# TensorE's eight passes over K and V written as one loop in the program, with V at one place and K turned into two fixed buffers

## The chip, the core and the metric

The kernel runs on one core of a Trainium2 chip. The metric is the device time of one execution in microseconds (us). Before the change it is 400.53 us (median of 3 runs, 400.43 to 400.56). All inputs lie in HBM and are read once; the result is one row of 1024 numbers.

## The reference, cut to what matters

A single token `x` (1 x 1024) goes through a layernorm, and the normed row `xn` then through two blocks whose results are added to `x`. Block A is attention of 32 query heads over a cache of 65536 keys in 4 groups (8 heads share a group's K and V); block B is a small MLP.

```python
q = (xn @ wq).reshape(B, Sq, Hq, Dh).transpose(0, 2, 1, 3)          # 32 heads of 128
scores = jnp.einsum("bhqd,bhkd->bhqk", q, k) * (Dh ** -0.5)         # k, v: 4 groups x 65536 x 128
o = jnp.einsum("bhqk,bhkd->bhqd", softmax(scores), v)
A = o.transpose(0, 2, 1, 3).reshape(B, Sq, Hq * Dh) @ wo
h = gelu(layernorm(xn) @ w1); x1 = xn + shifted(h) @ w2             # one token: every shift brings in zeros
B = x1 + gelu(layernorm(x1) @ w3) @ w4
return x + A + B
```

All arrays are bf16. K and V are 67.1 MB each, the weights together some 36 MB; the profile counts 169.87 MB read from HBM.

## The kernel before, in words

The kernel writes its program through a recorder (`Program`). Each call like `dve.transpose(...)` or `prog.load(...)` adds one `Op` to a list, with the regions that it reads and writes. `plan` then finds for each op which earlier ops it must wait for, and `emit` writes the instructions for every engine in that order: each engine executes its own ops in the order of the list, and waits on semaphores. A wait is attached to the instruction itself (the last of several; the others become separate wait instructions ahead of it, as do all waits of an instruction that accumulates). Because all goes through the recorder, VectorE's and ScalarE's instructions stand under one line in the profile (L82), loads from HBM under L89, weight loads of TensorE under L102, bf16 matmuls under L106 and f32 matmuls under L116 and L122.

The work is eight **turns** (u = 0 to 7), two for each of the four groups (g = u // 2, b = u % 2). A turn takes half a group's cache: 32768 keys, an 8.39 MB tile of K and as large a tile of V, each laid out as 128 partitions by 32768 bf16. A turn consists of:

- `scores(u)`: for each of four quarters of the K tile, VectorE transposes the quarter in 32 x 32 blocks, in place (128 x 4096 words), and TensorE runs 16 matmuls of it against `qdiag`, which holds the group's queries on its diagonal blocks, into `sc` (128 x 2048 f32 in PSUM). All 64 matmuls accumulate into the same four banks.
- `maxima(u)`: VectorE takes the maximum of each row of `sc`; TensorE turns the column of maxima into a row (`turn32`), VectorE reduces over the rows of one head, TensorE turns the result back, VectorE copies it to `nball`.
- `weights(u)`: ScalarE computes the exponential of `sc` into `p_sb` with the sums in `lall`, and VectorE transposes `p_sb`.
- `values(u)`: TensorE runs 64 matmuls of `p_sb` against the V tile into `oacc`.
- After the first turn of a group ScalarE copies `oacc` to `og` (`first_rows`). In the second turn VectorE weighs the two halves (`group_weights`, `group_rows`), a pair of f32 matmuls of `ol` against `selx` gathers the heads, and four small VectorE steps put the group's result into `oT`. These last steps stand on VectorE ahead of the next turn's first transpose.

Ahead of the turns stand the layernorms and the products with `wq`, `w3`, `w1` and `w2`; behind them the product with `wo` (64 matmuls from `oT`) and the one with `w4`, whose tile comes in five pieces, and the output.

All large loads are issued by SP in one queue, in the order wq, w3, w1, w2, K0, V0, K1, V1, ... K7, V7, wo, w4. SBUF holds three **slots** of 128 x 32768 bf16; the n-th tile of that stream has slot n % 3, and a load is recorded where the tile three places ahead in the stream has had its last use (`freed`):

```python
stream = ["wq", "w3", "w12"] + [(kind, u) for u in range(NU) for kind in "KV"] + ["wo", "w4"]
tiles = {it: slots[i % 3] for i, it in enumerate(stream)}
...
n = stream.index(it) + 3
if n < len(stream):
    load(stream[n])
```

So V of turn u+1 is issued when the scores of turn u are done, and K of turn u+2 when the values of turn u are done. The functions that the change touches are `Op`, `Program`, `load`, `scores`, `maxima`, `weights`, `values`, `first_rows`, `group_rows` and the loop over the turns at the end.

Of the kernel before, what the change touches and what calls it, by code (L numbers as in the profile page):

```python
# [14 lines left out]
P = 128  # L15
# [24 lines left out]
class Op:  # L40
    def __init__(self, engine, emit, reads, writes, alone=False, transfer=False):
        self.engine, self.emit, self.alone, self.transfer = engine, emit, alone, transfer
        self.reads = [region(a) for a in reads]
        self.writes = [region(a) for a in writes]
        self.waits = []
        self.awaited = False


class Program:

# [3 lines left out]
    def __init__(self, nc):  # L54
        self.nc = nc
        self.engines = {"pe": nc.tensor, "dve": nc.vector, "act": nc.scalar, "pool": nc.gpsimd, "sp": nc.sync}
        self.ops = []
        self.held = {}
        self.sems = []

    def add(self, op):
        for key in [k for k, (_, r) in self.held.items() if any(meet(r, w) for w in op.writes)]:
            del self.held[key]
        self.ops.append(op)
        return op

# [57 lines left out]
    def plan(self):  # L124
# [4 lines left out]
        for n, op in enumerate(self.ops):  # L129
# [21 lines left out]
            if e == "pool" and last_pool is not None:  # L151
                needs(last_pool, True)
            picked = sorted(need.values(), key=lambda o: o.n)
# [22 lines left out]
            for r in op.reads:  # L176
                readers.setdefault(r[0], []).append((r, op))

# [4 lines left out]
    def emit(self, first, last):  # L183

        if not hasattr(self, "queue_sems"):
            self.queue_sems = {e: self.sem(f"done_{e}") for e in ("pe", "dve", "act", "pool")}
            self.values = {e: 0 for e in self.engines}
        for n, op in list(enumerate(self.ops))[first:last]:
            e = self.engines[op.engine]
            waits = [(o.sem, o.value) for o in op.waits]  # L190
            ahead = waits if op.alone else waits[:-1]
            for s, v in ahead:
                e.wait_ge(s, v)
            ins = op.emit()
            if waits and not op.alone:
                ins.wait_op(waits[-1][0], waits[-1][1], "sem-ge")
            if op.transfer:
                op.sem, op.value = self.sem(f"landed_{n}"), 16
                ins.then_inc(op.sem, 16)
            elif op.awaited:  # L200
                self.values[op.engine] += 1
                op.sem, op.value = self.queue_sems[op.engine], self.values[op.engine]
                ins.then_inc(op.sem, 1)
# [3 lines left out]
def kernel(  # L207
# [42 lines left out]
    slots = [sb(f"slot{i}", [P, ROW], BF16) for i in range(3)]  # L250
# [34 lines left out]
    stream = ["wq", "w3", "w12"] + [(kind, u) for u in range(NU) for kind in "KV"] + ["wo", "w4"]  # L285
    tiles = {it: slots[i % 3] for i, it in enumerate(stream)}

    def load(it):
        t = tiles[it]
        if it == "wq":  # L290
            prog.load("sp", t[:], A_wq.rearrange("(p c) n -> p (c n)", c=DC))
# [5 lines left out]
        elif it == "wo":  # L297
            prog.load("sp", t[:], A_wo.rearrange("(p j) n -> p (j n)", p=P))
        elif it == "w4":
            w4_v = B_w4.rearrange("(m c) n -> m c n", c=FC)  # L300
            c0 = 0
            for n in W4_PIECES:
                prog.load("sp", t[:, c0 * D:(c0 + n) * D], w4_v[:, c0:c0 + n, :].rearrange("p c n -> p (c n)"))
                c0 += n
        else:
# [3 lines left out]
            prog.load("sp", t[:], cache[0, g, b * UKEYS:(b + 1) * UKEYS, :].rearrange("(p ct) d -> p (ct d)", p=P))  # L309

    def freed(it):

        n = stream.index(it) + 3
        if n < len(stream):
            load(stream[n])
# [24 lines left out]
    pool.memset(g_col[:], 0.0)  # L340

# [55 lines left out]

    def compute_wq():
        wt = tiles["wq"][:].rearrange("p (c h a i) -> p c h a i", c=DC, a=4, i=32)
        row_matmul(xn_rep, lambda c, i, a: wt[:, c, 16 * i:16 * (i + 1), a, :], (512, 512))  # L400
        freed("wq")
# [10 lines left out]
    def place_queries(g):  # L412
        for a in range(4):
            at = slice(32 * a, 32 * a + 32)
            pool.tensor_copy(
                out=qdiag[at, LEAD:].rearrange("p (x c) -> p x c", x=4)[:, :, 32 * a:32 * a + 8],
                in_=qx[at, :, 8 * g:8 * g + 8])

    def compute_w3():
# [3 lines left out]
        freed("w3")  # L423
# [6 lines left out]
    def compute_w12():  # L430
# [10 lines left out]
        freed("w12")  # L441

    W = ROW // SETS
# [12 lines left out]
    def scores(u):  # L456
        g, b = divmod(u, NB)
        if b == 0:
            place_queries(g)
        t = tiles["K", u]  # L460
        cols = t[:].rearrange("p (s u k b x r) -> p s u k b x r", u=SUBS, s=SETS, k=16, b=2, r=2)
        for s in range(SETS):
            words = t[:, W * s:W * (s + 1)].bitcast(F32)
            dve.transpose(out=words, in_=words)
            for b2 in range(2):
                for r in range(2):
                    c0 = LEAD + P * (2 * b2 + r) - 8 * s
                    for e in range(SUBS):
                        pe.mm(sc[:, e, :], qdiag[:, c0:c0 + P], cols[:, s, e, :, b2, :, r],
                              s == 0 and b2 == 0 and r == 0, s == SETS - 1 and b2 == 1 and r == 1)  # L470
        freed(("K", u))

    def maxima(u):
        g, b = divmod(u, NB)
        dve.reduce_max(out=mx[:], in_=sc[:].rearrange("p e n -> p (e n)"), axis=AX.X)
        at = next_pm()
        pe.turn32(at[0:1, 0:P], mx[:, 0:1], ident_f[:])
        dve.tensor_reduce(out=m8[:], in_=at[0:1, 0:P].rearrange("o (j h) -> o h j", h=8), axis=AX.X, op=ALU.max)
        dve.tensor_scalar(out=rep[:].rearrange("o (j h) -> o j h", h=8),
                          in0=m8[:].unsqueeze(1).to_broadcast([1, P // 8, 8]), scalar1=-SCALE, scalar2=None, op0=ALU.mult)  # L480
# [3 lines left out]
    def weights(u):  # L484
# [3 lines left out]
        dve.transpose(out=p_sb[:], in_=p_sb[:])  # L488

    def values(u):  # L490
        vt = tiles["V", u][:].rearrange("p (s u t d) -> p s u t d", u=SUBS, s=SETS, t=16)
# [5 lines left out]
        freed(("V", u))  # L497

    def first_rows():
        act.copy(out=og[:], in_=oacc[:])  # L500
# [8 lines left out]
    def group_rows(g):  # L509
        at = next_pm()  # L510
# [4 lines left out]
        pe.mm32(at[:, 0:DH + 1], selx[:], ol[:], True, True)  # L515
# [11 lines left out]
    for u in range(NU):  # L527
        g, b = divmod(u, NB)
        scores(u)
# [7 lines left out]
        else:  # L537
            group_rows(g)

# [77 lines left out]
```

## Time and profile before

| what | value |
|---|---|
| median of 3 runs | 400.53 us |
| the profiled execution, its own time | 400.43 us |
| its span, first to last instruction | 399.1 us |
| mean granted TensorE clock | 0.798 |
| TensorE busy (matmul) | 221.0 us, 55% |
| VectorE busy | 210.2 us, 53% |
| ScalarE busy | 27.6 us, 7% |
| HBM read | 169.87 MB, 426 GB/s over the span |
| one 128 x 4096 transpose of K | 4411 ns, 32 of them |
| one matmul of `scores` | 512 of them, 128.4 us busy in all |

The page names engines PE (TensorE matmul), PEld (TensorE weight load), DVE (VectorE), ACT (ScalarE), POOL (GpSimd) and SP. A timeline line gives the start within the span, the length, the engine, the line of the kernel, the operation, and in brackets how long the engine had been idle before and what released it. The lines of the queue that loads (SPq) give the time of the issue, not of the landing. The chain of waits goes from the last instruction back to what released it, and shows each piece with its start and its length; a DMA piece runs from the issue to the landing, so it includes the time that the transfer stands in the queue behind others.

### The profile page before, as it was taken

To read this page: it belongs to the slowest core of one execution; us is meant where nothing else is said; L and a number is where in the kernel's file an instruction comes from. 1 tells how busy PE (TensorE), PEld (TensorE's weight loads), DVE (VectorE), ACT (ScalarE), POOL (GpSimd) and SP (SyncE) were. 2 spreads that over 40 slices of the span, in tenths; PEclk is the share of its full clock that TensorE was granted. 3 is DMA by queue.
4 is the path that set the end of the run, shared out by engine and by line. 5 is a ranking of instruction groups with operands and counts; after the bars stand their busy time and mean duration, and the time that the engine had idled before them with its cause. 6 is when DMAs were issued, how large, how long until landed. Compare 5 with 4: busy or idle time off the path is not lost.

```text
span 399.1 us, 2559 instructions
## 1 busy us (share of the span) xinstructions
PE 221.0 (55%) x1360; PEld 45.5 (11%) x890; DVE 210.2 (53%) x156; ACT 27.6 (7%) x35; POOL 6.2 (2%) x29
## 2 busy tenths in 40 slices
PE   0250970592669246822874387429552946393586
PEld 0210010000201010011001100101010102010233
DVE  0520010975096549643963696359439932793411
ACT  1010030002000200020002000200010010002000
POOL 2000000000000000000000000000000000000000
PEclk9996895697659686968795679678966986597789
DMA  8989999999999999999999999999999999999996
GB/s 342 479 388 417 471 420 427 421 460 466 422 420 427 420 429 427 460 453 427 415 427 420 434 440 447 448 427 420 427 429 434 440 447 435 427 420 427 402 442 256
DMA packets 3760, 170.03 MB, mean 426 GB/s; under 512 B 419, under 2 KB 421, under 8 KB 678
## 3 DMA queue, kind: packets, MB, share of 16 engines
q1 hardware_dynamic: 3744, 169.87, 98.7%
q8 instruction: 9, 0.15, 0.1%
q14 instruction: 1, 0.01, 0.0%
q10 hardware_dynamic: 6, 0.00, 0.0%
HBM read 169.87 MB, written 0.00 MB: 426 GB/s over the span
## 4 chain that ended last, share of the span: by engine, by line
DMA 56%; DVE 21%; PE 17%; another core or an unknown queue 2%; ACT 2%; issue 0%; SPq 0%; POOLq 0%
DMA slot<-in_A_k_cache_dram 42%; DVE slot L82 15%; PE sc L106 12%; DMA slot<-in_B_w_dram 9%; DMA slot<-in_A_wq_dram 5%; PE oacc L106 4%; DVE p_sb L82 2%; DVE mx L82 2%; ACT p_sb L82 2%; PE pm L122 1%; DVE m L82 0%; DVE rep L82 0%; DVE nball L82 0%; DVE x_halves L82 0%
## 5 line engine op out<-in xcount | busy, mean ns | idle before, releaser
L82 DVE STREAM_TRANSPOSE slot<-slot 128x4096 f32<-128x4096 f32 x32 | 139.4, 4411 | 52.4 <-DMA slot<-in_A_k_cache_dram 52.3
L106 PE MATMUL sc<-slot,qdiag 128*128 128x512 bf16 x512 | 128.4, 410 | 69.7 <-DVE slot L82 69.6
L106 PE MATMUL oacc<-slot,p_sb 128*32 128x512 bf16 x512 | 44.9, 528 | 37.5 <-DVE negmg L82 18.8
L82 DVE STREAM_TRANSPOSE p_sb<-p_sb 128x2048 bf16<-128x2048 bf16 (+2 forms) x10 | 20.8, 2085 | 38.9 <-ACT p_sb L82 38.8
L82 DVE TENSOR_REDUCE mx<-sc 128x1 f32<-128x2048 f32 x8 | 18.3, 2292 | 29.7 <-PE sc L106 29.7
L102 PEld LDWEIGHTS <-qdiag 128*128 128x128 bf16 x128 | 13.0, 102 | 180.8 <-issue 180.8
L82 ACT ACTIVATE p_sb<-sc,nball 128x2048 bf16<-128x2048 f32 x8 | 15.7, 1967 | 250.7 <-DVE nball L82 250.7
L102 PEld LDWEIGHTS <-p_sb 128*32 128x32 bf16 x512 | 17.0, 128 | 62.1 <-issue 19.7
L106 PE MATMUL sc<-slot,ln_rep_b 128*32 128x512 bf16 (+1 forms) x80 | 16.2, 827 | 9.4 <-DMA slot<-in_B_w_dram 9.1
L82 DVE SCALAR_TENSOR_TENSOR og<-oacc,wb,og 128x512 f32<-128x512 f32 x4 | 3.0, 750 | 19.1 <-PE oacc L106 19.1
L122 PE MATMUL pm<-ident_f,mx 128*1 128x128 f32 x8 | 2.4, 296 | 19.1 <-DVE mx L82 19.1
L106 PE MATMUL psB<-slot,oT 128*32 128x512 bf16 x64 | 8.8, 443 | 1.3 <-DVE oT L82 1.3
L116 PE MATMUL pm<-ol,selx 128*128 128x129 f32 x8 | 2.3, 370 | 10.6 <-DVE ol L82 10.6
L82 DVE TENSOR_TENSOR og<-psB,slot 64x512 f32<-64x512 f32 x1 | 0.7, 683 | 13.8 <-PE psB L106 13.8
L106 PE MATMUL sc<-slot,ln_rep_a 128*32 128x512 bf16 x64 | 5.4, 512 | 4.5 <-DMA slot<-in_A_wq_dram 4.5
L116 PE MATMUL pm<-ln_rowsum_a,msk 128*128 128x1 f32 x2 | 0.6, 361 | 13.3 <-DVE ln_rowsum_a L82 13.3
L82 POOL COPY qdiag<-qx 32x32 bf16<-32x32 bf16 x16 | 3.2, 203 | 277.2 <-PE sc L106 251.1
L82 DVE STREAM_TRANSPOSE p_sb<-x_row 32x256 bf16<-32x256 bf16 x4 | 2.5, 616 | 7.4 <-DMA x_row<-in_A_x_dram 7.4
L106 PE MATMUL psB<-slot,hT 128*32 128x512 bf16 x40 | 4.7, 379 | 1.0 <-DMA slot<-in_B_w_dram 1.0
L122 PE MATMUL pm<-ident_f,rep 1*128 1x1 f32 x8 | 1.9, 240 | 5.0 <-DVE rep L82 5.0
L82 ACT COPY og<-oacc 128x512 f32<-128x512 f32 x4 | 2.3, 585 | 32.2 <-PE oacc L106 32.2
L102 PEld LDWEIGHTS <-ln_rep_b 128*32 128x32 bf16 x40 | 1.9, 112 | 22.9 <-issue 22.6
(86 smaller groups left out, 61.8 us busy)
## 6 DMA issues: line engine op xcount, KB each, us to landing
slot<-in_B_w_dram SPq DMA_DIRECT2D x1, 7168.0 KB, 37.4
slot<-in_B_w_dram SPq DMA_DIRECT2D x3, 2048.0 KB, 43.2
slot<-in_B_w_dram SPq DMA_DIRECT2D x1, 3072.0 KB, 33.8
slot<-in_B_w_dram SPq DMA_DIRECT2D x1, 1280.0 KB, 33.5
slot<-in_B_w_dram SPq DMA_DIRECT2D x1, 512.0 KB, 34.3
slot<-in_B_w_dram SPq DMA_DIRECT2D x1, 256.0 KB, 34.5
slot<-in_A_k_cache_dram SPq DMA_DIRECT2D x8, 42.1
slot<-in_A_v_cache_dram SPq DMA_DIRECT2D x8, 36.9
```

The source lines that it names most:

```text
L82: return program.add(Op(engine, lambda: method(*args, **kw), reads, writes, alone=kw.get("accum_out") is not None))
L102: self.add(Op("pe", lambda: pe.ldweights(lhsT, tile_position=pos), [lhsT], []))
L106: return pe.add_instruction(mybir.InstMatmult(name=nc.get_next_instruction_name(), engine=mybir.EngineType.PE, start_tensor_calc=start, st ...
L116: return self.add(Op("pe", lambda: pe.matmul(out, lhsT=lhsT, rhs=rhs, start=start, stop=stop, tile_position=pos, skip_group_check=True), [ ...
L122: return self.add(Op("pe", lambda: pe.transpose(out, in_, identity), [in_, identity], [out]))
```

## The change

TensorE's share of the eight turns becomes one loop in the program, executed eight times (`Fori` on TensorE alone, its first instruction put at the start of a block of 256 instructions). Its body has 221 instructions: 131 matmuls, 80 weight loads, 8 semaphore instructions and the two of the loop. The other engines' programs stay written out.

For this every turn must read and write the same addresses on TensorE, and its waits must not name a turn:

- V has one place, so V of turn u+1 is recorded after `values(u)`.
- VectorE no longer transposes K in place: it writes quarter i of a turn to `turned[i % 2]`, one of two fixed quarter-size buffers.
- K has two places that share their second and first half. The shared half is read first in even turns (`QUARTERS`) and as it lies in odd ones, so K of turn u+1 can be issued after the second quarter's matmuls of turn u. `wo` takes the place of K after the second quarter of turn 7, `w4` is issued after its scores.
- A wait of TensorE within the loop is a separate semaphore instruction ahead of the use (`taken`), which waits for 1 (16 for a load) and subtracts it again. There are eight per turn: four transposes, the maxima, the row of maxima, the turned `p_sb`, and the landing of V.
- The f32 matmuls of `ol` against `selx` stand at the head of every turn, behind the take of the first transpose, and once behind the loop. The four small VectorE steps behind them (`group_out`) stand behind the second transpose of the next group's first turn.
- ScalarE's copy of `oacc` to `og` is made in two halves; the maxima always use the same PSUM bank.

```diff
+    def taken(self, other):
+        other.mailed = True
+        def emit():
+            n = 16 if other.transfer else 1
+            return self.engines["pe"].add_instruction(mybir.InstEventSemaphore(
...
+                    on_wait=[mybir.SyncWait(sync_type="semaphore", id=other.sem.num, ant_name=other.sem.name,
+                                            wait_mode="sem-ge-imm", wait_value=n)],
+                    on_update=[mybir.SyncUpdate(sync_type="semaphore", id=other.sem.num, ant_name=other.sem.name,
+                                                update_mode="sem-sub-imm", update_value=n)])))
+        return self.add(Op("pe", emit, [], [], take=other))
...
+            with self.nc.Fori(0, len(self.turns), engines=[pe], head_slot={pe: 0}):
+                for op in self.turns[0]:
+                    self.put(op)
...
-    slots = [sb(f"slot{i}", [P, ROW], BF16) for i in range(3)]
+    HALF, W = ROW // 2, ROW // SETS
+    space = sb("space", [P, 3 * ROW], BF16)
...
-    tiles = {it: slots[i % 3] for i, it in enumerate(stream)}
+    tiles = {"wq": space[:, 0:ROW], "w3": space[:, 2 * ROW:3 * ROW], "w12": space[:, ROW:ROW + HALF],
+             "wo": space[:, 0:ROW], "w4": space[:, ROW:2 * ROW], "V": space[:, 2 * ROW:3 * ROW],
+             "K": [space[:, 0:ROW], space[:, HALF:HALF + ROW]]}
+    turned = [space[:, 3 * HALF + W * i:3 * HALF + W * (i + 1)] for i in range(2)]
+    QUARTERS = [(2, 3, 0, 1), (0, 1, 2, 3)]
...
-        for s in range(SETS):
-            words = t[:, W * s:W * (s + 1)].bitcast(F32)
-            dve.transpose(out=words, in_=words)
+        for i, s in enumerate(QUARTERS[b]):
+            turn = dve.transpose(out=turned[i % 2].bitcast(F32), in_=tiles["K"][b][:, W * s:W * (s + 1)].bitcast(F32))
...
+            prog.taken(turn)
+            if i == 0:
+                pe.mm32(pm[1][:, 0:DH + 1], selx[:], ol[:], True, True)
...
+            if i == 1:
+                seen = prog.ops[-1]
+                load(("K", u + 1) if u + 1 < NU else "wo").after.append(seen)
+                if b == 0 and g:
+                    group_out(g - 1)
+        if u + 1 == NU:
+            seen = prog.ops[-1]
+            load("w4").after.append(seen)
...
     def values(u):
-        vt = tiles["V", u][:].rearrange("p (s u t d) -> p s u t d", u=SUBS, s=SETS, t=16)
+        prog.taken(loaded[u])
+        vt = tiles["V"].rearrange("p (s u t d) -> p s u t d", u=SUBS, s=SETS, t=16)
...
-        freed(("V", u))
+        if u + 1 < NU:
+            loaded.append(load(("V", u + 1)))
```

## The prediction, made before the changed kernel had run

> **What bounds the kernel now.** I read the page's DMA rows first, then the chain that ended last, then SP's own timeline (its times are when a transfer is issued), and last one turn's timeline.
>
> ```profile
> DMA packets 3760, 170.03 MB, mean 426 GB/s; under 512 B 419, under 2 KB 421, under 8 KB 678
> q1 hardware_dynamic: 3744, 169.87, 98.7%
> q8 instruction: 9, 0.15, 0.1%
> ```
>
> The transfer engines are busy 98.7% of the span, TensorE 55% and VectorE 53%. The transfers set the time; compute matters only where it makes them wait.
>
> The next lines are from the chain: start, length, what. A transfer's length runs from issue to landing.
>
> ```profile
> 0.88 21.88 DMA slot<-in_A_wq_dram
> ...
> 28.27 41.86 DMA slot<-in_A_k_cache_dram
> ...
> 144.14 42.29 DMA slot<-in_A_k_cache_dram
> ...
> 222.04 41.79 DMA slot<-in_A_k_cache_dram
> ...
> 298.28 42.95 DMA slot<-in_A_k_cache_dram
> ```
>
> K lands at 70.13 (turn 0), 186.43 (turn 3), 263.83 (turn 5) and 341.23 (turn 7). From turn 3 to turn 7 four pairs of K and V pass in 154.80 us, so one transfer of 8.39 MB takes D = 19.35 us in a full queue. The first transfer, into an empty queue, took A = 21.88 us from issue: restarting costs A - D = 2.53 us. By the same step K of turn 1 lands at 109.0 (its first transpose starts at 109.04).
>
> SP's timeline tells how early the queue is refilled:
>
> ```profile
> 91.28 0.33 SPq L89 DMA_DIRECT2D slot<-in_A_v_cache_dram  x1
> 105.84 0.33 SPq L89 DMA_DIRECT2D slot<-in_A_k_cache_dram  x1
> 130.18 0.33 SPq L89 DMA_DIRECT2D slot<-in_A_v_cache_dram  x1
> 144.14 0.33 SPq L89 DMA_DIRECT2D slot<-in_A_k_cache_dram  x1
> ```
>
> With three slots, turn 1 (K landed at 109.0) issues V of turn 2 after its scores, 21.1 us later, and K of turn 3 after its values, 35.1 us later. At the first of these issues, 130.18, the queue still holds work until K of turn 2 lands at 147.7, 17.5 us; at the second, 144.14, until V of turn 2 lands at 167.1, 23 us.
>
> Now one turn, from its timeline:
>
> ```profile
> 109.04 17.42 DVE L82 STREAM_TRANSPOSE slot<-slot 128x4096 f32<-128x4096 f32 x4 [9.66 <-DMA slot<-in_A_k_cache_dram]
> 113.54 16.61 PE L106 MATMUL sc<-slot,qdiag 128*128 128x512 bf16 x64 [7.75 <-DVE slot L82]
> 119.28 0.10 PEld L102 LDWEIGHTS <-qdiag 128*128 128x128 bf16 x1 [0.95 <-issue]
> 146.73 0.49 PE L116 MATMUL pm<-ol,selx 128*128 128x129 f32 x2 [2.64 <-DVE ol L82]
> ```
>
> Four transposes run back to back, 4.34 us apart. The first quarter's 16 matmuls are slow (fifth weight load at 119.28, so the second quarter starts at 119.5, 10.46 us into the turn), while TensorE, after its idle time, runs on a lowered clock (granted 0.75 on average from 109 to 148); later quarters take 3.5 us. Nobody waits for the slow one today: the transposes are in place.
>
> **The change part by part.** *V at one place.* V of turn u+1 can be issued only when values(u) has ended, not after the previous scores. Call S the start of a turn's first transpose, E the issue at the end of its values; E - S before is, from SP's issues and the transposes' starts, 35.69, 35.10, 34.22, 35.59, 34.28, 34.43, 35.56, 35.06. At E the queue holds only K of turn u+1, which lands 2D = 38.7 us after K of turn u. So V keeps the queue full only if E - S is at most 38.7 - 2.53 = 36.2, with S at K's landing. Before, the longest is 35.69: the cover shrinks from 17 us to about 1 us. Nothing else hides this, since there is one queue and it bounds the kernel.
>
> *K's places share half.* K of turn u+1 is issued after the second quarter's matmuls, 13.9 us into the turn. It has until V of the turn lands at 19.35 less 2.53: 2.9 us of cover left. Free. K stands ahead of V in SP's queue and never waits for something later. wo follows by the same rule (free), and w4 after scores(7), some 17 us before wo lands (free).
>
> *K turned into two fixed buffers.* A transpose of the same shape, priced at 4.40 us as now. The trace has none out of place at this size. Of the near rows, the 128x2048 one of p_sb, in place, took 2312 ns, 1.13 ns a column, and the 32x256 one out of x_row 616 ns, 2.4 ns a column, but it is short and reads with a stride; I take the present 1.08 ns a column, the shape being the same. At 2.4 ns the four transposes would take 21 us more per turn and decide everything; that end is left to the last rival. But the third transpose overwrites what the first quarter's matmuls read, and now waits for them. They end at 9.29 to 10.46 us into the turn (second quarter's start in the eight turns, mean 9.77), where the third transpose used to start at 8.69. In addition the fixed body opens every turn with the two f32 matmuls of ol against selx (0.49 us above) between the first transpose and the first quarter. So the third transpose starts 9.77 + 0.5 - 8.69 = 1.6 us later, and the fourth and last quarter with it. Bounds: 0.9 (9.29, half of the f32 work absorbed as the clock rises) and 2.7 (10.46, f32 at half clock, 0.9). The DVE steps of group_out now stand behind the second transpose, 1.0 us inside that wait: hidden. In exchange they leave the gap before the next even turn: S is E + 2.6 (0.75 + 0.69 + 1.02 of group_rows and gaps), not E + 4.05.
>
> *The loop and its takes.* Eight semaphore instructions per turn, each of them a wait and a decrement ahead of a weight load. The first transpose's is counted in the 0.5 above; four more stand on the path: fourth transpose, mx, rep, turned p_sb. ScalarE's exponential already has a separate wait and starts 0.03 us after its releaser; a weight load, formerly ahead of the wait, costs 0.10. I take 0.1 each, 0.4 in all; bounds 0.3 (most of them at the weight load alone) and 0.6 (both, with 0.02 to spare). Behind each take stand that step's matmuls, and for them wait DVE, then SP. The back edge is hidden: after E, TensorE waits at least 4.45 us for the first turned quarter.
>
> *Sum.* E - S grows by 1.6 + 0.4 = 2.0 us (1.2 to 3.3). Turn by turn, with K(u+1) landing D after V(u), V(u+1) landing at the later of K(u+1) + D and E + A, and S the later of K's landing + 0.02 and, on even turns, E + 2.6:
> turn 0: S 70.15, E 107.84, V lands 129.72 instead of 128.36: gap 1.36.
> turn 1: S 109.03, E 146.13, V would be in time (168.01 against 168.42): none.
> turn 2: S 149.09, E 185.31: gap 0.07. Turn 3: S 187.79, E 225.38: gap 1.37.
> turn 4: S 227.98 (E + 2.6), E 264.26: 0.18. Turn 5: 0.10. Turn 6: S 305.66, E 343.22: 1.46.
> Together 4.5 us. A gap lengthens the next turn's cover, hence the alternation. After V of turn 7 nothing can run dry; the closing matmuls come 5.1 us later, the last weights 4.5 us later, and the 1.02 us that TensorE waits for w4 now covers the difference. The profiled execution took 400.43 (span 399.1 and 1.33 around it; the median of the runs is 400.53): 400.43 + 4.5 = 405.0.
>
> A is one row, taken in an empty chip; the lower end is the closing 2 KB store, issued at 397.95 and ended with the span 1.15 us later. With A = 20.5 the sum is 0.4, with A = 21.88 and 1.2 or 3.3 us per turn it is 1.8 or 9.7. I take 21.88, the only row of a transfer of this size. The Trainium skill, "DMA: Bandwidth & Descriptors", section "Anatomy of one DMA", fits a GpSimd-issued transfer as about 2.0 us fixed and bytes at 436 GB/s; as an estimate that is 21.2 us here, so nearly the row, and by it the sum would be 2.6 and the time 403.0.
>
> **The rivals.** *The cover holds* (not slower): if restarting costs 1.2 us instead of 2.53, the limit on E - S is 37.5 and seven turns stay within about 0.2 of it; 400.4 to 400.9. It decides at E - S = 38.7 less the restart. For it: only one empty-queue row exists. Against: that row.
>
> *Fewer code fetches* (faster): the nine instruction packets took 0.1% of 16 x 399.1 us, about 0.7 us each (0.35 to 1.06 by rounding), on engines that are full. A loop needs perhaps four. If the ones saved sit on the engine that ends last, 1 us is gained: 399.4. Against: K lands at equal steps (77.40 and 77.40 us) with fetches in both, so they do not add up on one engine.
>
> *The takes or the back edge are dear*: at 0.5 us a take on the path, E - S grows by 3.6 and the sum by the same steps is 11: 411. It leaves the forecast's range from about 0.4 us a take. If the loop's code were fetched again at each back edge, the fetch would have to exceed the 4.45 us of idle TensorE before it decides; 8 us would make E - S 5.5 longer in all, and the sum 23: 423. Transposes at 2.4 ns a column would do more still. The body is 221 instructions and starts at a block of its own, which speaks against. The Trainium skill, "Runtime: NRT & Kernel Launch", section "Instruction fetch mechanics", warns that a taken branch to code outside the two blocks held must fetch first; the nine packets of 16 KB agree with its block size, and no run here shows a branch.
>
> *The change does not do what it says* is excluded: the program order shows TensorE's 221-instruction loop and the one V place.
>
> **How the numbers follow.** Forecast (gaps, +1 to +10) 0.70, at 405.0; cover holds 0.14; fewer fetches 0.06; dear takes or back edge 0.10. The range is 400.3 (A = 20.5, short wait) to 410.0 (3.3 us per turn); left out are 0.06 below and about 0.10 above. A measurement of this kernel tells 0.2%, 0.8 us, from no change. Faster 0.06; within 0.2%: 0.14; slower 0.80.
>
> **What would show it.** Right: SP's V issues 36.2 to 37.8 us after the first transpose; third transposes starting 10.3 us into a turn with a wait for TensorE; GB/s dips where V starts; gaps after turns 0, 3, 6 larger than after 1, 2, 5; K landings 77.4 us apart only where no gap falls. Wrong: V issued within 36 us and the time still longer (another cause), transposes slower than 4.4 us, or TensorE's first matmul more than 0.3 us behind the first transpose of a turn.

## The result, and the profile after

The changed kernel takes **409.68 us** (median of 6 runs, 408.59 to 415.2), the kernel before 400.49 us beside it (6 runs, 400.39 to 400.56). The run of 415.2 was disturbed and is left out of the comparison, as are one of 592.7 us of `both` and one of 424.0 us of `no_loop` further below. The ratio of the others is **1.0224 [1.0207, 1.0241]**, some 9.0 us slower. The profiled execution took 408.59 us against 400.43, so 8.16 us more. Forecast were 405.0 us in a range of 400.3 to 410.0: the sign is right, the loss is about twice what was forecast, and the time lies only 0.3 us inside the range.

The page of the changed kernel, its rows of DMA and of the transposes (busy us and mean ns of one; idle us before them):

```profile
span 407.3 us, 2669 instructions
...
q1 hardware_dynamic: 3744, 169.87, 97.4%
q8 instruction: 3, 0.05, 0.0%
...
L114 DVE STREAM_TRANSPOSE space<-space 128x4096 f32<-128x4096 f32 x32 | 140.3, 4424 | 58.9 <-DMA space<-in_A_k_cache_dram 47.0
...
space<-in_A_k_cache_dram SPq DMA_DIRECT2D x8, 25.6
space<-in_A_v_cache_dram SPq DMA_DIRECT2D x8, 22.2
```

The transposes out of place cost what those in place did (4424 against 4411 ns), and only three packets of code are fetched. What moved is the last two rows: from issue to landing V takes 22.2 us (36.9 before) and K 25.6 (42.1 before). V's 22.2 us are hardly more than the 21.88 us that the first transfer of all took into an empty queue: V now starts with the queue empty or nearly so. SP's timeline shows why:

```profile
109.05 0.33 SPq L121 DMA_DIRECT2D space<-in_A_v_cache_dram  x1
123.36 0.33 SPq L121 DMA_DIRECT2D space<-in_A_k_cache_dram  x1
146.91 0.33 SPq L121 DMA_DIRECT2D space<-in_A_v_cache_dram  x1
164.39 0.33 SPq L121 DMA_DIRECT2D space<-in_A_k_cache_dram  x1
```

V of turn 1 is issued at 109.05 and K of turn 1, the only work in the queue, lands at 109.13 by the trace's DMA records. V lands at 130.79, 21.74 us after its issue. The windows view around that issue (engine times, then the granted clock, the DMA share and GB/s by where packets start) shows where the packets stop and start again:

```profile
107.00:109.00 2.00, 2.00 (x28) 0.70 (x20) 0.00 (x0) 0.00 (x0) 0.00 (x0) 0.76 0.00 0
109.00:111.00 2.00, 0.01 (x3) 0.00 (x0) 1.85 (x1) 0.65 (x2) 0.00 (x0) 1.00 1.49 524
```

No data packet starts from 107 to 109, while TensorE is still busy with the values for all of the 2 us. The transfer engines are not idle for all of that time: by the DMA records a 64 KB packet takes 2.42 us, the last packets of K end on the 16 engines from 107.02 to 108.79, and the first of V start from 110.00 to 110.99. So an engine has nothing to move for 2.4 us on average, and V lands 2.31 us later than it would in a full queue. Turn 1 in the timeline (start, length; in brackets the idle time and its releaser):

```profile
109.15 8.77 DVE L114 STREAM_TRANSPOSE space<-space 128x4096 f32<-128x4096 f32 x2 [6.57 <-DMA space<-in_A_k_cache_dram]
...
113.75 0.77 PE L148 MATMUL pm<-ol,selx 128*128 128x129 f32 x2 [4.74 <-PEq L90]
...
114.31 9.02 PE L138 MATMUL sc<-space,qdiag 128*128 128x512 bf16 x32
...
119.89 8.77 DVE L114 STREAM_TRANSPOSE space<-space 128x4096 f32<-128x4096 f32 x2 [1.97 <-PE sc L138]
...
134.91 0.27 PE L154 MATMUL pm<-ident_f,mx 128*1 128x128 f32 x1 [2.48 <-PEq L90]
...
141.06 5.81 PE L138 MATMUL oacc<-space,p_sb 128*32 128x512 bf16 x64 [4.93 <-PEq L90]
```

Two transposes where four ran back to back; the third waits 1.97 us for the first quarter's matmuls (`PE sc L138`), which stand behind the f32 pair. A take shows as `PEq L90`.

### The profile page after: what moved, and what is told of

Read it like the earlier page. It is cut to its first block, busy times and chain, and to the rows that moved or that the text cites. A ratio compares the mean times of both kernels' runs of the same rounds, so it can differ in the third digit from the quotient of the medians.

```text
span 407.3 us, 2669 instructions
## 1 busy us (share of the span) xinstructions
PE 226.3 (56%) x1370; PEld 50.6 (12%) x900; DVE 211.2 (52%) x156; ACT 27.9 (7%) x39; POOL 6.5 (2%) x30
## 5 line engine op out<-in xcount | busy, mean ns | idle before, releaser
L114 DVE STREAM_TRANSPOSE space<-space 128x4096 f32<-128x4096 f32 x32 | 140.3, 4424 | 58.9 <-DMA space<-in_A_k_cache_dram 47.0
L138 PE MATMUL sc<-space,qdiag 128*128 128x512 bf16 x512 | 129.5, 411 | 14.9 <-PEq L90 14.9
L138 PE MATMUL oacc<-space,p_sb 128*32 128x512 bf16 x512 | 46.0, 538 | 39.4 <-PEq L90 39.4
L148 PE MATMUL pm<-ol,selx 128*128 128x129 f32 x18 | 6.9, 489 | 65.9 <-PEq L90 63.3
L134 PEld LDWEIGHTS <-p_sb 128*32 128x32 bf16 x512 | 19.3, 129 | 62.9 <-issue 59.7
L138 PE MATMUL sc<-space,ln_rep_b 128*32 128x512 bf16 (+1 forms) x80 | 16.2, 828 | 9.6 <-DMA space<-in_B_w_dram 9.4
L148 PEld LDWEIGHTS pm<-ol,selx 128*128 128x128 f32 x18 | 4.5, 311 | 71.7 <-issue 68.5
L138 PE MATMUL psB<-space,oT 128*32 128x512 bf16 x64 | 9.4, 464 | 1.2 <-DVE oT L114 1.2
L138 PE MATMUL sc<-space,ln_rep_a 128*32 128x512 bf16 x64 | 5.2, 496 | 4.6 <-DMA space<-in_A_wq_dram 4.6
L114 ACT COPY og<-oacc 128x256 f32<-128x256 f32 x8 | 2.6, 375 | 33.9 <-PE oacc L138 33.9
## 6 DMA issues: line engine op xcount, KB each, us to landing
space<-in_B_w_dram SPq DMA_DIRECT2D x3, 2048.0 KB, 43.4
space<-in_A_k_cache_dram SPq DMA_DIRECT2D x8, 25.6
space<-in_A_v_cache_dram SPq DMA_DIRECT2D x8, 22.2
```

What stands on the lines that cost most here:

```text
L114: return program.add(Op(engine, lambda: method(*args, **kw), reads, writes, alone=kw.get("accum_out") is not None))
L134: self.add(Op("pe", lambda: pe.ldweights(lhsT, tile_position=pos), [lhsT], []))
L138: return pe.add_instruction(mybir.InstMatmult(name=nc.get_next_instruction_name(), engine=mybir.EngineType.PE, start_tensor_calc=start, st ...
L148: return self.add(Op("pe", lambda: pe.matmul(out, lhsT=lhsT, rhs=rhs, start=start, stop=stop, tile_position=pos, skip_group_check=True), [ ...
```

## The measured sum

With S the first transpose of a turn and E the issue at the end of its values, E - S is 38.68, 37.76, 37.65, 36.77, 37.40, 36.65, 37.35, 38.99 us in turns 0 to 7 (the last one to the end of the values): mean 37.66, against 34.99 before. Into an empty queue V takes 21.74, 21.80, 21.78 and 21.72 us (turns 1, 3, 5, 7; forecast 21.88). The DMA records of the trace give each landing; what a landing comes later than 19.35 us after the one ahead is a gap:

```
gap at V of turn            1     2     3     4     5     6     7    total
after (us)               2.31  0.05  1.33  0.00  1.27  0.00  1.14   6.1
forecast                 1.36  0.00  0.07  1.37  0.18  0.10  1.46   4.5
```

With A = 21.76 us as measured, no landing of K or V in the turns of the changed kernel is over 0.15 us later than the forecast's own rule gives it from its issue and the landing ahead. So the rule held here; the sizes put into it did not. wo lands at 386.20 instead of 379.93.

The last 2 us come from the end. The chain of the changed kernel (start, length, what):

```profile
379.08 6.29 PE oacc L138 x63
...
390.02 13.44 PE psB L138 x101
...
403.75 0.69 DVE og L114
...
405.13 0.50 PE pm L138 x12
405.63 0.02 issue
405.65 0.43 DVE x_halves L114
```

Before, the chain ended on the landing of w4 (397.08 us), and TensorE waited 1.02 us for it. Now TensorE and VectorE alone carry the end. The values of turn 7 end at 385.3, 9.1 us later than before (376.25): turn 7 starts 5.1 us later and lasts 3.9 us longer. 9.1 less the 1.02 us of waiting is 8.1, the 8.16 us of the profiled execution. The last weights are no help either: they land at 404.96, 7.9 us late, 6.3 by the gaps and 1.5 by a packet of code fetched at 394.4, behind which one piece of w4 lands 8.86 us after the landing ahead instead of 7.31 before.

## The experiments

Two theories were set against each other: the loss is the emptied queue, through V's late issue and the longer turn together (the forecast); or it is the loop itself, its takes and its branch. All kernels compute the reference in full. "us over" is (ratio - 1) x 400.5, so that kernels run on different occasions compare.

| kernel | what it is | ratio to before | us over |
|---|---|---|---|
| after | the change | 1.0224 [1.0207, 1.0241] | 9.0 |
| t_wait | before + transposes wait for matmuls | 1.0027 [1.0015, 1.0039] | 1.1 |
| v_late | before, V recorded later | 1.0000 [0.9990, 1.0009] | 0.0 |
| both | the two edits above | 1.0022 [1.0007, 1.0038] | 0.9 |
| v_after | before + V waits for the values | 1.0111 [1.0086, 1.0137] | 4.4 |
| both_after | v_after + t_wait | 1.0252 [1.0235, 1.0269] | 10.1 |
| no_loop | after, turns written out | 1.0318 [1.0293, 1.0343] | 12.7 |
| no_takes | no_loop, waits attached | 1.0235 [1.0220, 1.0250] | 9.4 |
| straddle | after, loop body over two blocks | 1.0210 [1.0195, 1.0225] | 8.4 |
| pm_late | after, f32 pair later in the turn | 1.0174 [1.0150, 1.0198] | 7.0 |
| halves | pm_late, V in two halves | 1.0188 [1.0171, 1.0205] | 7.5 |
| eighths | pm_late, K turned in eighths | 1.0057 [1.0036, 1.0078] | 2.3 |
| eighths_flat | eighths, written out | 1.0097 [1.0082, 1.0111] | 3.9 |

### One edit at a time in the kernel before

**t_wait**: the third and fourth transposes wait for the matmuls of the first and second quarter.

```diff
-            dve.transpose(out=words, in_=words)
+            turn = dve.transpose(out=words, in_=words)
+            if s >= 2:
+                turn.after.append(ends[s - 2])
...
+            ends.append(prog.ops[-1])
```

> The kernel before, with the third and fourth transposes of a turn made to wait for the matmuls of the first and second quarter, as two fixed buffers would make them; all else as before, three slots. Theory: the turns grow by 0.7 to 1.8 us, the transfers have 17 us of cover and do not notice; only the last turn's growth of 1.8 us reaches the end, less 1.0 us of slack there: 400.8 to 401.6 us. Rival (the longer turn costs by itself, wherever the loads are issued): 8 times 1.1 us, 409.

Measured 401.80 us, 1.1 us over by the ratio and at the upper end of what was expected. The landings of K and V are those of before and the last weights still land at 397.04, although E - S is 36.4 to 38.2 us (mean 37.0): with V issued after the scores, 12 to 16 us before the queue would run dry, the queue doesn't notice. Only the end does; its chain:

```profile
372.28 6.26 PE oacc L107 x62
...
383.19 13.14 PE psB L107 x50
...
398.28 0.49 PE pm L107 x12
398.80 0.43 DVE x_halves L83
```

The values of turn 7 end at 378.5 instead of 376.25. 2.25 us less the 1.02 us for which TensorE waited at the end before is 1.2, and its span is 1.3 us longer. The same rule for the end holds in the changed kernel.

**v_late** and **both**: V's load is only recorded later, behind the values, in the kernel before and in t_wait.

```diff
-        freed(("K", u))
+        if u + 1 == NU:
+            freed(("K", u))
...
+        if u + 1 < NU:
+            freed(("K", u))
         freed(("V", u))
```

> The kernel before, with one thing changed: V of the next turn (with K of the turn after it, as the slots allow) is issued after the values of a turn, not after its scores. Theory (the transfers run dry only when a turn's values end later than 36.3 us after its first transpose, the sum of two transfers, 38.7 us, less the 2.4 us by which a transfer into an empty queue takes longer, 21.75 against 19.35 us): the turns stay at 34.2 to 35.7 us, no gap opens, 400.4 to 400.9 us. Rival (V at one place costs by itself): 404 or more.

> The two edits together (V issued after the values, third and fourth transposes waiting), no loop, no takes, the f32 matmuls where they were. Theory: turns of 35.2 to 36.9 us against a limit of 36.3, small gaps of 0.5 to 0.8 us in three or four turns, and 0.5 to 0.8 at the end: 402 to 403.5 us, more than the two alone add up to. Rival (edits add): the sum of the two losses alone, 401.5 or less under the theory's own values.

Both failed as experiments. Their 400.45 and 401.54 us, though near what was expected, are those of the kernel before and of t_wait, because the issue did not move: a load waits for the last use of its place, not for its place in the list, and in the profile V is still issued at 92.04 and 130.39. `both` only repeats t_wait.

**v_after** makes V wait for the last matmul of the values:

```diff
+        if u + 1 < NU:
+            seen = prog.ops[-1]
+            freed(("K", u))
+            prog.ops[-1].after.append(seen)
         freed(("V", u))
```

> The kernel before, with V of the next turn made to wait for the last matmul of the turn's values (K of the turn after it follows at once). This is the edit that v_late did not make: there SP issued V after the scores as before. Theory: the turns stay at 34.2 to 35.9 us, under the limit of 36.3, so no gap: 400.4 to 401.0 us. Rival (V issued late costs by itself): 404 or more.

Measured 404.85 us, 4.4 us over: **a miss**, the most useful one. Its page and SP's timeline:

```profile
q1 hardware_dynamic: 3744, 169.87, 98.3%
q8 instruction: 9, 0.15, 0.1%
```

```profile
104.59 0.33 SPq L90 DMA_DIRECT2D slot<-in_A_v_cache_dram  x1
104.96 1.06 SPq L90 DMA_DIRECT2D slot<-in_A_k_cache_dram  x1
144.64 0.33 SPq L90 DMA_DIRECT2D slot<-in_A_v_cache_dram  x1
```

V is issued 4.4 and 3.2 us before the K ahead of it lands (108.96, 147.83), in time by the forecast's limit of 2.5, and E - S is 34.2 to 35.8. (How long a load is issued before the work ahead of it lands is its cover.) Yet wo lands 4.4 us late. The DMA records say where. Call excess what a landing comes later than both 19.35 us after the landing ahead and 21.76 us after its own issue:

```
transfer      landed   excess   code fetched at
V, turn 1     128.49   0.18     -
V, turn 2     168.41   1.23     146.3
V, turn 3     207.76   0.65     201.0
V, turn 5     285.48   0.16     -
K, turn 6     305.86   1.02     299.1
K, turn 7     345.07   0.51     343.1
wo            384.35   0.71     382.3
```

4.1 of the 4.4 us fall on transfers during which a packet of code was fetched. (The two V's among them also have little cover, so the fetch need not be all of their excess.) In the kernel before nine packets are fetched as well, and no K or V from turn 2 on has an excess of over 0.02 us. It is not the cover of the late transfer itself that differs: the two K's and wo in the table were issued 21.5 to 23.7 us ahead. What differs is told behind the last run.

**both_after**: v_after and t_wait together, in the kernel before, with no loop and no take. Its diff is those two.

> V waiting for the values, and the third and fourth transposes waiting for the first and second quarter's matmuls, in the kernel before; no loop, no takes, f32 matmuls where they were. Theory: with the turns of t_wait (36.4 to 38.2 us) and the limit of 36.3, gaps of 0.4 to 2 us in most turns, 5.5 to 6.5 in all, plus up to 1 at the end, and up to 4 more if code fetches land in a queue without cover as in no_loop: 405.5 to 411 us. Rival (the edits add): 401.5 to 402, the sum of the two alone.

Measured 410.31 us, 10.1 over, in the range of the theory. The sum fits, its parts do not: wo lands 8.1 us late, and of the gaps in its records only 1.8 us are V's started into a queue that was empty or nearly so, for which 5.5 to 6.5 were expected. Another 6.5 are excesses, nearly all on transfers with a fetch, for which at most 4 were allowed. The two edits cost 4.4 and 1.1 alone; together they cost nearly twice their sum.

### The loop and its takes

**no_loop**: the same program with TensorE's turns written out. The takes stay.

```diff
-            with self.nc.Fori(0, len(self.turns), engines=[pe], head_slot={pe: 0}):
-                for op in self.turns[0]:
-                    self.put(op)
             for op in ops[head:]:
-                if op.turn is None:
-                    self.put(op)
+                self.put(op)
```

> The kernel after, with TensorE's eight turns written out instead of a loop; the takes, the one place of V, the two buffers and the f32 matmuls at the head of a turn stay. Theory: the back edge is hidden behind the wait for the first transpose, so the time is that of the kernel after, 408.5 to 410.5 us. Rival (the loop's branch or the fetch of its code is what costs): 405 us or less.

It is 12.7 us over, 3.8 us **slower** than with the loop; neither theory had it. Its page:

```profile
span 413.0 us, 2651 instructions
...
q1 hardware_dynamic: 3744, 169.87, 96.4%
q8 instruction: 9, 0.15, 0.1%
```

Nine packets of code again instead of three. In the changed kernel they come at 44.0, 58.7 and 394.4 us, none of them in the turns; here at 106.8, 149.1, 211.1, 255.2, 302.8, 347.9 and so on. K of turn 2, during the one at 149.1, has an excess of 1.68 us, V of turn 3, at 211.1, one of 1.28. Of 8.9 us of excesses in all, some 4.5 fall on transfers with a fetch; the other 4.4 fall on transfers with none, most of them a V issued with under 2.5 us of cover (2.05 us at V of turn 7). These go with the spread of the engines, that is how far apart the 16 engines end the same transfer: ahead of the V's of turns 5 to 7 it is 1.8 to 2.0 us here, and in the changed kernel, where V's with as little cover have no excess, 0.4 to 0.7 from turn 1 on. The rival "fewer code fetches" named a real gain. It has a value here because the change has emptied the queue.

**straddle** puts the head of the loop in the middle of a block, so that the body lies in two.

```diff
-            with self.nc.Fori(0, len(self.turns), engines=[pe], head_slot={pe: 0}):
+            with self.nc.Fori(0, len(self.turns), engines=[pe], head_slot={pe: 128}):
```

> The kernel after with one number changed: the loop's first instruction stands at slot 128 of a block of 256 instructions, so that its 221 instructions lie in two blocks. Nothing that is computed or waited for changes. Theory (code is fetched block by block through the same transfer engines, and in a queue without cover each fetch of 16 KB makes one engine, and so the whole transfer, about 1 us later): fetches once or more per turn, 10 to 16 instruction packets instead of 3, 412 to 418 us. Rival (both blocks stay held; no fetch): 3 or 4 packets, 408.5 to 410.5 us.

Measured 408.50 us, no slower than the change: the theory is **missed**, and the rival has it. The page:

```profile
span 407.2 us, 2669 instructions
...
q8 instruction: 3, 0.05, 0.0%
```

Three packets for eight passes: nothing is fetched again at the back edge, with the body in one block or in two. The Trainium skill, "Runtime: NRT & Kernel Launch", section "Instruction fetch mechanics", says that a taken branch must fetch when its target lies outside the two blocks held. The row agrees: with the body within two blocks nothing is fetched at the back edge. The same section calls the cost of passing from block to block mostly hidden and names branches as a reason for writing code out. Here the measurements differ: the loop is 3.8 us faster than the same code written out, and a fetched block is seen in the landings.

**no_takes**: no_loop with each wait attached to the instruction that uses the data, as in the kernel before. The f32 pair is then no longer behind the take of the first transpose and runs early, so the price is that of the takes and of the pair together.

```diff
     def taken(self, other):
 
-        other.mailed = True
+        return
```

> no_loop with TensorE's waits attached to the instructions again, so no takes; all else as in no_loop. Theory: turns 0.4 to 0.6 us shorter, and so the time 2 to 3 us below no_loop's 413.7: 410.5 to 412 us. Rival (the takes cost nothing): 413 to 414.5 us.

Measured 410.02 us, a little below the expected 410.5; 9.4 us over, 3.3 less than no_loop. In sum it stands within 1 us of both_after (10.1), the same two edits in the kernel before. That the parts agree too is not shown: here K is issued some 5 to 9 us ahead, there 21 to 24 from turn 2 on.

Along the kernels measured, a path of four steps leads from before to after: V late +4.4, the transposes' wait on top +5.7, takes, the f32 pair and the rest of the order +2.6, the loop -3.8; unrounded they add up to 9.0.

### Giving the turn its time back

**pm_late**: the f32 pair behind the second quarter, `group_out` behind the fourth transpose.

```diff
             prog.taken(turn)
-            if i == 0:
-                pe.mm32(pm[1][:, 0:DH + 1], selx[:], ol[:], True, True)
...
                 load(("K", u + 1) if u + 1 < NU else "wo").after.append(seen)
-                if b == 0 and g:
-                    group_out(g - 1)
+                pe.mm32(pm[1][:, 0:DH + 1], selx[:], ol[:], True, True)
+            if i == 3 and b == 0 and g:
+                group_out(g - 1)
```

> The kernel after, with the f32 matmuls of ol against selx moved from the head of a turn to behind the second quarter's matmuls, where TensorE waits anyway, and group_out behind the fourth transpose. Theory: turns 0.5 to 0.65 us shorter, gaps smaller by 2 to 2.6 us: 406.5 to 408 us. Rival (this work is hidden where it is): unchanged, 409 to 410.

Measured 408.03 us, just above what was expected; 7.0 over. The first quarter of turn 1 starts 4.59 us into the turn instead of 5.16.

**halves**: pm_late with V loaded in two halves, the first as soon as half of the values is done. The pieces read from HBM become 8 KB long.

```diff
-        if u + 1 < NU:
-            loaded.append(load(("V", u + 1)))
+            if u + 1 < NU and e % 2:
+                loaded[u + 1].append(load(("V", u + 1), e // 2))
```

> pm_late, and V loaded in two halves (source runs of 8 KB), the first of them issued when half of the values' matmuls are done, some 2.9 us earlier; TensorE takes both at once. Theory: the limit on a turn rises from 36.3 to about 39, no gaps remain, only the last turn's growth is paid at the end: 401 to 403 us. Rival (the place of V is not what costs, or the smaller runs slow the transfers): 406 or more.

Measured 407.75 us, 7.5 over: the first theory's 401 to 403 is **missed**, and the rival has it. Its page:

```profile
span 404.6 us, 2677 instructions
...
q1 hardware_dynamic: 11040, 169.87, 98.9%
```

The queue is as busy as before the change (98.9% against 98.7%), but with 11040 packets for 3744. A V in halves takes 19.87 us in a full queue instead of 19.35, and eight times 0.52 us are 4.2 of the 5.5 that its profiled execution (405.88) is over: the gaps are closed and most of the time is lost in the transfers. Another 1.1 us is one excess, at the first half of V of turn 7, which was issued 4.0 us ahead of the landing before it, with no fetch near it.

**eighths**: pm_late with K turned in eighths into four buffers of half the size. A transpose then overwrites what was read four transposes ago.

```diff
-    turned = [space[:, 3 * HALF + W * i:3 * HALF + W * (i + 1)] for i in range(2)]
+    W2 = W // 2
+    turned = [space[:, 3 * HALF + W2 * i:3 * HALF + W2 * (i + 1)] for i in range(4)]
...
-        for i, s in enumerate(QUARTERS[b]):
-            turn = dve.transpose(out=turned[i % 2].bitcast(F32), in_=tiles["K"][b][:, W * s:W * (s + 1)].bitcast(F32))
+        for i in range(2 * SETS):
+            at = W * QUARTERS[b][i // 2] + W2 * (i % 2)
+            turn = dve.transpose(out=turned[i % 4].bitcast(F32), in_=tiles["K"][b][:, at:at + W2].bitcast(F32))
```

> pm_late with K turned in eighths instead of quarters, into four buffers of half the size in the same space; TensorE starts after 2.2 us of a turn instead of 4.4, a transpose waits for the matmuls of four eighths earlier, and after the last transpose only half a quarter's matmuls are left. The loop has 241 instructions, in one block. Theory: no transpose waits, the values end 33 to 34.5 us into a turn, which is inside the limit even for the engines that lead by 2 us (38.7 - 2.0 - 2.4 = 34.3), so the queue stays full: 399.5 to 401 us, that is, all of the 9 us are back, with the loop, the takes and the one place of V still there. Rival (the loop and its takes, or the one place of V as such, cost): 404 or more.

Measured 402.56 us (401.14 to 404.4), above the expected 399.5 to 401, and 2.3 over. Turn 1, SP's issues and the DMA rows of the profiled execution:

```profile
108.88 17.66 DVE L114 STREAM_TRANSPOSE space<-space 128x2048 f32<-128x2048 f32 x8 [10.63 <-DMA space<-in_A_k_cache_dram]
...
111.34 9.59 PE L138 MATMUL sc<-space,qdiag 128*128 128x512 bf16 x32 [7.08 <-PEq L90]
```

```profile
104.30 0.33 SPq L121 DMA_DIRECT2D space<-in_A_v_cache_dram  x1
...
142.39 0.33 SPq L121 DMA_DIRECT2D space<-in_A_v_cache_dram  x1
...
182.24 0.33 SPq L121 DMA_DIRECT2D space<-in_A_v_cache_dram  x1
```

```profile
q1 hardware_dynamic: 3744, 169.87, 98.7%
q8 instruction: 4, 0.07, 0.1%
```

The eight transposes run back to back, TensorE starts 2.5 us into the turn instead of 4.6, and E - S falls to 33.3 to 34.7 us although there are four takes more. The queue is at 98.7% again. With V still at one place and the loop still there, 6.7 of the 9.0 us are back: the loss was the length of the turn. What remains in the profile, 1.3 us at wo, is two excesses, 0.80 at V of turn 3 and 0.65 at V of turn 5, which were issued 4.0 and 3.9 us ahead of the landing before them. The V's of the other five turns, 4.6 to 5.4 us ahead, have none.

**eighths_flat**: eighths, written out as in no_loop.

> eighths with the eight turns written out instead of the loop (some nine code fetches again). Theory: with cover in the queue a code fetch costs next to nothing, so within 1 us of eighths, 399.5 to 402 us, while without cover the same step cost 4 us (no_loop against the kernel after). Rival (a code fetch costs the same everywhere): 3 to 5 us above eighths.

3.9 us over, 1.6 more than with the loop, between the two expectations. In its records two excesses are large: 1.52 us at K of turn 4 (a fetch at 220.0) and 1.30 at K of turn 7 (338.0); four other fetches in the turns (102.1, 142.9, 181.8, 262.1) cost 0.1 us or less. The 16 engines end such a transfer 1.98 us apart ahead of the first of the two and 3.51 us apart behind it. One engine fell back by 1.5 us, and the landing is that of the last engine.

What a fetch costs can be read from all these runs together. Each row has a transfer with one fetch; the spread is that of the landing ahead of it.

```
kernel, transfer        cover   spread   fetched at   excess
before, K, turn 5       22.43    2.06      249.6       0.00
v_after, K, turn 6      21.54    0.71      299.1       1.02
both_after, K, turn 2   21.48    0.61      148.1       1.68
both_after, K, turn 5   21.48    0.63      254.7       1.21
both_after, K, turn 7   23.60    1.50      347.5       0.76
eighths_flat, K, turn 2  8.13    1.87      142.9       0.01
eighths_flat, K, turn 4  7.72    1.98      220.0       1.52
```

With the same 21 to 24 us of cover a fetch costs nothing or up to 1.7 us. The spread decides: in the kernel before, each of the seven fetches from 104.6 to 378.5 us sets one more engine some 1.5 us back, which is seen in the sorted times of the 16 engines. But one engine is already 2 us behind the first, so the last landing stays where it is (the fetch at 104.6 moves it by 0.18). The first fetch, at 43.4 us, found the engines 0.56 us apart: w1 landed 6.19 us after the landing ahead, and w2, which is of the same size and comes next, took 4.90. There the kernel before paid 1.3 us as well, in a full queue. A start into an empty queue brings the engines level again (1.78 us apart ahead of V of turn 1 in the changed kernel, 0.53 behind it), and the next fetch shows. And where the engine that is set back is the last one already, as at 220.0 (1.98 us behind the first, then 3.51), it shows all the same.

## Why the prediction was right or wrong, point by point

- **V at one place: the mechanism was right.** V was issued into an emptied queue, its price into an empty one was 21.72 to 21.80 us (forecast 21.88), and large gaps alternate with small ones, although in other turns than forecast.
- **"The cover shrinks from 17 us to about 1 us" and costs nothing by itself: failed**, but not through the limit of 36.2 us. v_after keeps E - S below it and loses 4.4 us, 4.1 of them where code is fetched. The failed step is the one that priced code fetches at nothing because "K lands at equal steps with fetches in both". That they do not add up on one engine was right; but the steps were equal because one engine was 2 us behind already, and after a V that starts late the engines are level (0.71 us apart ahead of K of turn 6 in v_after) and a fetch costs 1.0 us. In the changed kernel it did no harm to the forecast, since the loop fetches nothing in the turns.
- **E - S grows by 2.0 us: mis-sized, 2.67** (2.48 over turns 0 to 6, the ones that a V follows). The third transpose comes 1.97 us later (10.66 us into the turn against 8.69; forecast 1.6), because the f32 pair holds the first quarter back by 0.65 us instead of 0.5 and the quarter itself, at a lowered clock (granted 0.50 from 114 to 118 us in turn 1), takes 5.5 us instead of 5.3 before. The takes cost 0.09, 0.09, 0.09 and 0.23 us over the gaps of before: 0.5 (forecast 0.4). The last is the take of the turned `p_sb`, 0.29 us from the transpose's end to the matmul. Fed with the measured E - S, the forecast's rule gives 6.3 us of gaps for the measured 6.1. The term that was too small is this one, and near the limit a little more length costs much more gap.
- **The end covers the difference: failed.** The closing matmuls were to come 5.1 us later and the weights 4.5. They came 9.1 and 7.9 us later: 5.0 us of gaps ahead of turn 7 (forecast 3.1), 3.9 us more of turn 7 (forecast 2.0), and for the weights a fetch of 1.5 us that was costed at nothing. The 1.02 us of waiting was consumed as said, and TensorE sets the end: 8.1 us. That the time still lies inside the range is luck: its upper end was worked out for turns longer by 3.3 us, and with the growth measured the forecast's own rule gives 6.3 us, so 406.7; the rest is the end, which in the forecast adds nothing.
- **K's shared half is free, the transposes cost the same, the back edge is hidden: right.** K is issued 13 to 15 us into the turn and has no excess of over 0.15 us; 4424 ns; straddle.
- **The rivals.** *The cover holds* fell with the restart of 2.4 us. *The takes or the back edge are dear* fell: 0.09 to 0.23 us a take. *Fewer code fetches* was right in direction and, in this queue, bigger than its 1 us: 3.8 us between no_loop and after, 1.6 between eighths_flat and eighths. It lies inside the loss. A fetched packet took 1.02 to 1.10 us in the kernel before, not some 0.7, and sets its engine back by 1.5. The 423 us for a back edge of 8 us do not follow from the steps given: 5.5 us more in every turn give 18.5 us of gaps, so 419.

**What stays open.** The profiled execution is 8.16 us over, the ratio of the runs makes it 9.0; the kernels with little cover scatter by 1 to 3 us from run to run where the kernel before scatters by 0.2 to 0.6, and only profiled executions were decomposed. That fetches cost time in these kernels is shown by the two pairs with and without the loop; that a fetch does so by holding back one engine is read from the sorted landings, and no run changed the spread alone. The records used do not name the engine. Nor is it settled why a transfer issued into a nearly empty queue can come later than both limits with no fetch near it: 0.65 and 0.80 us at 3.9 and 4.0 us of cover (eighths), 1.94 us at 2.0 (V of turn 3 in pm_late), yet 0.16 at 2.3 (V of turn 5 in v_after). In the profiles all such excesses of over 0.4 us have this in common: the cover less the spread ahead, that is the cover of the engine that leads, is under the 2.4 us of a restart (4.0 less 1.7 in eighths). Others below 2.4 have none, so it is a condition and not the cause. No run was made on it. No kernel of these beat the kernel before.

## What to carry to other kernels

When a kernel that is bound by its transfers gives up a buffer, work out for every issue how long before the queue runs dry it comes, against the turn as it will be with all that the change adds to it, and ask for some 5 us rather than the bare restart of 2.4, since the engines that lead run dry up to some 2 us earlier: here a few tenths in each turn became 6 us of gaps. A cost that does not show in the landings, such as fetched code in the kernel before, need not be small: look at when each engine ends, not only at the last one, or bound the cost by its own size. And check the end of the program apart: there the last turn's whole growth counts, not only the gaps.

## What the runs showed of the hardware that was not expected

- A fetched packet of code (16 KB) sets one of the 16 transfer engines some 1.5 us back, and the engine stays back until the queue runs empty or nearly so. The transfer lands late by as much as this engine passes the one that was last: 1.0 to 1.7 us where the engines were 0.5 to 0.7 us apart (v_after, both_after), at most 0.01 us in the kernel before from turn 2 on, where they are 2.06 apart.
- After a restart into an empty queue the 16 engines of the changed kernel end a transfer 0.4 to 0.7 us apart; in the kernel before, whose queue does not run dry, they stay 2.06 us apart from turn 1 on.
- The same 8.39 MB in runs of 8 KB take 19.87 us instead of 19.35, 2.7% more, with the queue equally busy.
- A wait that stands as an instruction of its own ahead of TensorE's weight load costs 0.15 us from the releaser's end to the matmul (0.29 at the values) where an attached one costs 0.05 to 0.06.
